# Third batch onward in one stated order for all engines, with a third PSUM bank for the first product and squares on ScalarE

## The chip, the cores and the metric

The kernel runs on one core of a Trainium2 chip. The metric is the device time of one execution in microseconds (us), the median of several runs. The engines are TensorE (PE; its weight loads are listed apart as PEld), VectorE (DVE), ScalarE (ACT), GpSimd (POOL) and SyncE (SP, which issues nearly all DMAs). Each executes its own instructions strictly in order and waits on semaphores for the others.

## What is computed

```python
q_s = softmax of q over the head dimension; k_s = softmax of k over the sequence
kv  = einsum('bhsd,bhse->bhde', k_s, v)
x   = einsum('bhsd,bhde->bhse', q_s, kv), heads side by side    # 4608 x 512
h   = x @ w_in;  g = relu(h) ** 2                               # 4608 x 2048
out = g @ w_out                                                 # 4608 x 512
```

The sizes are 8 batches, 8 heads, 576 positions, head dimension 64, all in fp32.

## The kernel before

**Tiling.** The 4608 rows of x are nine blocks of 512: 512 positions of each of the eight batches (blocks 0 to 7), and 64 left over of each batch, collected in block 8. A batch's eight heads are four pairs of two. Attention for a batch runs while the block before it is multiplied. Every fp32 product is made of three: both operands are split into a high and a low part (`copy` to fp32r on ScalarE, subtraction of the copy on GpSimd or VectorE), and high x high, high x low, low x high are added in PSUM.

**Blocks 0 and 1** take the first product as it stands (`h_part`), then relu, square, split (`relu`, `square`, `g_high`, `g_low`) and the second product (`out_part`). The order in block 0 is a list of tokens (`ORDER`). In block 1 a loop over 32 half steps runs `ffn_h` and `ffn_out`, and `put(at, ...)` hangs other work on half steps; only emission order is given, and a scheduler sorts the instructions of each engine from there on (`e.free()`).

**Blocks 2 to 8** use Strassen's scheme (Winograd's form) for the first product: eight *beats* a block, in each of which a 256-column pair of feature chunks is made of seven products (`PRODUCTS`), each six matmuls of 128x256. Their left sides are sums of w_in, made in block 1 (`w_sums`), kept in DRAM as `w_prod`; 14 stay in SBUF and the rest come through a ring of four tiles of two products. Their right sides are sums of x (`x_sums`: quarters B11 to B22, sums T1 to T4), each split in two (`x_split`). Between the products stand the second product's groups `o` of three 128x512 matmuls (`out_part`), eight a beat, which use the g of one and two beats ago. `BEAT` is this order.

The seven products go into two banks: X (bank 1) takes A11, S2, S3, A22 one upon the other, Y (bank 3) takes a copy of X after A11, then A12, and afterwards S1 and S4:

```python
def added(dst):     # after S1 with c[1][:, 1], after S4 with c[0][:, 1]
    e.dve.tensor_tensor(dst, dst, Y, op=ALU.add)
    e.dve.scalar_tensor_tensor(out=dst, in0=dst, scalar=0.0, in1=dst, op0=ALU.max, op1=ALU.mult)
def squared(dst, ps):   # after A12 with c[0][:, 0], Y; after A22 with c[1][:, 0], X
    e.act.activation(dst, ps, AF.Relu)
    e.dve.tensor_tensor(dst, dst, dst, op=ALU.mult)
```

`parts` then splits c into g: a cast on ScalarE, a subtraction on GpSimd.

**Attention of a pair** (`attention`): `k_max` (maximum of k over the sequence, with transposes and small reductions, on VectorE), `k_sub`, `k_exp`; `q_sub`, `q_exp`, `q_norm` (maximum, subtraction, exponential, sum, division, all but the exponential on VectorE), then a transpose `tb`, which goes to DRAM (`bounce_out`, one DMA) and comes back reordered as qT (`bounce_in`, four DMAs); `kv` (small matmuls), `rs`, `rr`, `kf`, `kv_high`, `kv_low` (its division and split); `q_high` and `q_low` (split of qT, ScalarE and GpSimd); and four products `attn`, each one matmul into a PSUM bank, an ACT copy `xf` of one half and DVE adds that write `x_raw`. `next_bank("a")` alternates between banks 0 and 7 for these and for kv. From batch 2's third pair on the two pairs of a half block are set off at fixed half steps (`TWO_AT`). In blocks 2 to 8 the matmuls are chained in the order of emission; the other engines' instructions are placed by the scheduler.

Of the kernel before, what the change touches and what calls it, by code (L numbers as in the profile page):

```python
# [31 lines left out]
BEAT = "A11 o o S2 A12 o o S3 o S1 o A22 o S4 o".split()  # L32
X_LOW_DVE = ("T2", "T3", "T4"), ("T3", "B22")
# [90 lines left out]
def attention_ffn_kernel(ctx: ExitStack, tc: tile.TileContext, q, k, v, w_in, w_out, out):  # L124
# [285 lines left out]
    def attention(b, pr, two):  # L410
# [43 lines left out]
        def q_norm():  # L454
            qn = st["qn"]
            qv = qn.rearrange("p j h d -> p (j h) d")
            qs = attn_pool.tile([P, LOW * 2, 1], F32, name="qs", tag=f"qs{n % NB}")
# [8 lines left out]
            e.dve.tensor_tensor(qv, qv, qs.broadcast_to([P, LOW * 2, D]), op=ALU.mult)  # L466
# [64 lines left out]
        def attn(g0, nj, h):  # L531
            def go():
# [8 lines left out]
                e.act.copy(corr[half[h]], ps[HALF:])
                e.dve.tensor_tensor(x[half[h]], ps[:HALF, :, :HIGH], corr[half[h], :, :HIGH], op=ALU.add)
                if nj == LOW:
                    e.dve.tensor_tensor(left[half[h]], ps[:HALF, :, HIGH], corr[half[h], :, HIGH], op=ALU.add)
                if nj == LOW and h == 1:
                    dst = x_left[:, pr, b * LEFT : (b + 1) * LEFT].rearrange("p (g a) -> p g a", g=2)
                    e.sp.dma_start(dst, left)
# [426 lines left out]
```

## Time and profile before

| | us |
|---|---|
| median of 3 runs (lowest, highest) | 939.71 (937.15, 939.99) |
| the profiled execution, its own time | 940.78 |
| its span in the trace | 939.0 |
| blocks 0 and 1 | 0 to 237 |
| blocks 2 to 5 (attention for batches 3 to 6, and part of the next) | 237 to 659.7 |
| block 6 (attention for batch 7) | 659.7 to 752.6 |
| blocks 7 and 8 (no attention) | 752.6 to 925.8 |
| last second-product groups and stores | 925.8 to 939 |

A block starts with its first A11 product. All of the kernel's instructions are issued by one helper (line 104 there, line 148 after the change), so groups are told apart by their tiles: `bank<-x_T,wp` and `bank<-x_B,wp` are the seven products (T1 to T4, and quarters of x), `bank<-wo,g` the second product, `bank<-vt,kt` the kv matmuls, `bank<-qs,kvs` the attention products, `c` and `g` what becomes of the first product, `qn`, `m`, `kt`, `xf`, `x_raw` steps of attention. A row of a stretch has its length in us, then for PE, PEld, DVE, ACT and POOL the busy us and the number of instructions, the mean granted share of TensorE's clock, the mean share of the DMA engines and GB/s. A row of a timeline has start and length in us, engine, operation, `out<-in`, size, count, and in brackets the idle time before it with its releaser. Matmuls overlap in the trace, so a PE row is longer than its share of PE's time.

### The profile page before, as it was taken

To read this page: it belongs to the slowest core of one execution; us is meant where nothing else is said; L and a number is where in the kernel's file an instruction comes from. 1 tells how busy PE (TensorE), PEld (TensorE's weight loads), DVE (VectorE), ACT (ScalarE), POOL (GpSimd) and SP (SyncE) were. 2 spreads that over 40 slices of the span, in tenths; PEclk is the share of its full clock that TensorE was granted. 3 is DMA by queue.
4 is the path that set the end of the run, shared out by engine and by line. 5 is a ranking of instruction groups with operands and counts; after the bars stand their busy time and mean duration, and the time that the engine had idled before them with its cause. 6 is when DMAs were issued, how large, how long until landed. Compare 5 with 4: busy or idle time off the path is not lost.

```text
span 939.0 us, 15774 instructions
## 1 busy us (share of the span) xinstructions
PE 870.0 (93%) x5422; PEld 733.5 (78%) x5422; DVE 674.5 (72%) x1392; ACT 454.4 (48%) x981; POOL 416.2 (44%) x350
## 2 busy tenths in 40 slices
PE   8999999997888988989899988988899999999998
PEld 6787878775777877877777777877788888888886
DVE  7998889889986789587877789597875553243332
ACT  4888845544653545445453545444544432243232
POOL 4577746667441363325341463326343432252222
PEclk9999999998899999999999999999999999999999
DMA  9989529877766744676466754676456544552552
GB/s 218 267 222 296 144 62 286 280 225 246 206 170 200 215 139 117 194 217 186 136 171 188 223 144 117 198 225 186 125 164 187 165 129 141 174 157 68 178 164 62
DMA packets 131663, 168.82 MB, mean 180 GB/s; under 512 B 51200, under 2 KB 95232, under 8 KB 131328
## 3 DMA queue, kind: packets, MB, share of 16 engines
q1 hardware_dynamic: 130832, 166.87, 62.0%
q8 instruction: 43, 0.70, 0.3%
q10 hardware_dynamic: 752, 0.95, 0.3%
q14 instruction: 36, 0.29, 0.1%
HBM read 134.74 MB, written 33.03 MB: 179 GB/s over the span
## 4 chain that ended last, share of the span: by engine, by line
PE 45%; DVE 30%; DMA 11%; issue 6%; ACT 4%; SPq 2%; POOL 1%; DVEq 0%; ACTq 0%; POOLq 0%
PE bank L104 45%; DVE c L104 6%; DVE m L104 5%; DMA qt<-in_q_dram 5%; DVE x_raw L104 3%; DMA kt<-in_k_dram 2%; SPq L104 2%; DVE qn L104 2%; DVE qm L104 2%; DVE kt L104 1%; DVE tb L104 1%; DMA wp<-w_prod 1%; DMA vt<-in_v_dram 1%; DVE x_T L104 1%; DVE T L104 1%
## 5 line engine op out<-in xcount | busy, mean ns | idle before, releaser
L104 PE MATMUL bank<-wo,g 128*128 128x512 f32 x1344 | 366.7, 396 | 0.0
L104 POOL TENSOR_TENSOR g<-c,g 128x512 fp32r<-128x512 f32 x112 | 147.5, 1318 | 338.6 <-ACT g L104 263.4
L104 PEld LDWEIGHTS bank<-wo,g 128*128 128x128 f32 x1344 | 232.3, 190 | 29.8
L104 PEld LDWEIGHTS bank<-x_T,wp 128*128 128x128 f32 x1344 | 186.8, 189 | 59.5 <-ACT bank L104 39.8
L104 PE MATMUL bank<-x_T,wp 128*128 128x256 f32 x1344 | 201.6, 286 | 22.9 <-ACT bank L104 20.3
L104 PE MATMUL bank<-x_B,wp 128*128 128x256 f32 x1008 | 152.4, 287 | 27.6 <-DVE c L104 27.5
L104 PEld LDWEIGHTS bank<-x_B,wp 128*128 128x128 f32 x1008 | 138.6, 192 | 43.5 <-DVE c L104 36.3
L104 DVE TENSOR_TENSOR c<-c 128x256 f32<-128x256 f32 x112 | 62.4, 557 | 93.3 <-ACT c L104 89.6
L104 POOL TENSOR_TENSOR qs<-qT,qs 64x640 fp32r<-64x640 f32 x48 | 80.6, 1678 | 90.8 <-ACT qs L104 81.3
L104 ACT CAST g<-c 128x512 fp32r<-128x512 f32 x112 | 69.5, 620 | 104.4 <-DVE c L104 103.8
L104 ACT ACTIVATE c<-bank 128x256 f32<-128x256 f32 x112 | 42.9, 383 | 114.3 <-PE bank L104 113.9
L104 DVE TENSOR_TENSOR c<-c,bank 128x256 f32<-128x256 f32 x112 | 46.5, 415 | 66.3 <-PE bank L104 65.9
L104 PE MATMUL bank<-x_hi,wi 128*128 128x512 f32 x256 | 88.2, 402 | 0.1
L104 DVE SCALAR_TENSOR_TENSOR c<-c 128x256 f32<-128x256 f32 x112 | 83.9, 749 | 2.8
L104 ACT COPY c<-bank 128x256 f32<-128x256 f32 x112 | 41.5, 371 | 91.5 <-PE bank L104 75.8
L104 PE MATMUL bank<-wo,g_hi 128*128 128x512 f32 x256 | 81.3, 401 | 0.0
L104 PEld LDWEIGHTS bank<-x_hi,wi 128*128 128x128 f32 x256 | 48.6, 190 | 11.5 <-DVE r L104 0.8
L104 PEld LDWEIGHTS bank<-wo,g_hi 128*128 128x128 f32 x256 | 47.8, 192 | 10.1 <-ACT g_hi L104 0.4
L104 PE MATMUL bank<-x_lo,wi 128*128 128x512 f32 x128 | 50.4, 394 | 0.0
L104 PE MATMUL bank<-wo,g_lo 128*128 128x512 f32 x128 | 49.9, 395 | 0.0
L104 DVE TENSOR_REDUCE m<-kt 128x128 f32<-128x640 f32 x32 | 41.9, 1308 | 8.4 <-DMA kt<-in_k_dram 8.1
L104 DVE TENSOR_REDUCE qm<-qt 128x10 f32<-128x640 f32 x32 | 25.9, 810 | 27.1 <-DMA qt<-in_q_dram 26.9
(122 smaller groups left out, 1190.3 us busy)
## 6 DMA issues: line engine op xcount, KB each, us to landing
wp<-w_prod SPq DMA_DIRECT2D x130, 512.0 KB, 3.8
wp<-w_prod SPq DMA_DIRECT2D x44, 256.0 KB, 3.0
out_dram<-o SPq DMA_DIRECT2D x68, 128.0 KB, 2.4
raw_i<-in_moe_w_in_dram SPq DMA_DIRECT2D x16, 512.0 KB, 7.7
raw_o<-in_moe_w_out_dram SPq DMA_DIRECT2D x16, 512.0 KB, 7.1
w_prod<-w_sum SPq DMA_DIRECT2D x32, 256.0 KB, 3.0
bounce<-tb SPq DMA_DIRECT2D x24, 320.0 KB, 2.2
qT<-bounce SPq DMA_DIRECT2D x96, 80.0 KB, 3.2
```

Of the source, the lines that this page charges most:

```text
L104: ins = f(*args, **kwargs)
```

## The change

- `BLOCK` is a list of tokens that states, for one block, the order of everything, and all five engines are chained to it from block 2 on. `name.j` is a step of beat j, `name/p` a step of attention of pair p (for the next batch), `x:` a step of the sums of x (`T` a sum, `h` a high part, `l` a low part), `w` a ring load, `ev`/`st` the taking out and storing of a finished output tile, `L` a load; `+` belongs to the block after, `-` to the one before. `AHEAD` hangs the first steps of batch 3 on half steps of block 1.
- S1 and S4 go to a third bank Z (bank 7), and S4 moves behind the next beat's A11 and two groups `o`. kv and all four attention products of a pair, for batches 3 to 7, share bank 0.
- `added` and `squared` become: `a22` (add to c, DVE), `r22` and `q22` (relu and square on ScalarE); `a12` (DVE adds c to Z in PSUM), `r12` (relu, ScalarE), `m12` (c times Z, DVE); `r11` (relu, ScalarE), `m11` (c times Y, DVE); `r21`, `q21` (relu and square, ScalarE). In block 1 the squares of 14 of 16 chunks go to ScalarE.
- For pairs from batch 2's third on, q's subtraction and q's division move from VectorE to GpSimd; from block 3 on all low parts of x are on GpSimd (before, T3 and B22 were on VectorE).
- `w_prod` is laid out in the order of use, so that every ring load is one DMA.

```diff
-BEAT = "A11 o o S2 A12 o o S3 o S1 o A22 o S4 o".split()
-X_LOW_DVE = ("T2", "T3", "T4"), ("T3", "B22")
+BEAT = "A11 o o S4 S2 o A12 o S3 o S1 o A22 o o".split()
+X_LOW_DVE = ("T2", "T3", "T4")
+Z_BANK = 7
...
+BLOCK = """
...
+a22.1 kv/1 r21.1 o12.1 Lv/3 r22.1 kp/1 kr/1 q21.1 o13.1 kh/1 A11.2 q22.1 kl/1 o00.2 c1.2 B/1 h1.1 o01.2 l1.1 S4.1
+Lk/3 S2.2 a12.1 qd/2 o02.2 r12.1 w4 u2.2 m12.1 A12.2 qh0/1 km/2 o03.2 Lq/0+ qh1/1 ql0/1 S3.2 k1/2 qx/2 o10.2 w5 h0.1
...
+P3/1 o02.3 u2.3 c3/1 A12.3 r12.2 d3/1 B/2 m12.2 o03.3 r11.3 x:T1 h0.2 S3.3 qm/3 l0.2 o10.3 w8 u3.3 m11.3 S1.3 qd/3
+qh0/2 kv/2 w9 a22.3 qh1/2 o11.3 Lv/0+ kr/2 A22.3 r22.3 ql0/2 kh/2 o12.3 o13.3 r21.3 Lq/1+ kl/2 kp/2 qx/3 A11.4 ql1/2
...
+""".split()
...
     def next_bank(who):
+        if who == "z":
+            return rest[2]
...
-            e.dve.tensor_tensor(
+            (e.pool if two else e.dve).tensor_tensor(
                 st["qn"].rearrange("p j h d -> p h j d"), qq, qm.broadcast_to([P, 2, LOW, D]), op=ALU.subtract
             )
...
-            e.dve.tensor_tensor(qv, qv, qs.broadcast_to([P, LOW * 2, D]), op=ALU.mult)
+
+        def q_scale():
+            qv, qs = st["qn"].rearrange("p j h d -> p (j h) d"), st["qs"]
+            (e.pool if two else e.dve).tensor_tensor(qv, qv, qs.broadcast_to([P, LOW * 2, D]), op=ALU.mult)
...
+            def times():
+                st[key] = next_bank("z" if b > 2 else "a")[:, : 2 * nj * BLK]
...
     def square(s):
         near = NFC <= s["blk"] * NFC + s["fc"] < NFC + LAG
+        if s["blk"] and not near:
+            e.act.activation(s["r"], s["r"], AF.Square)
+            return
...
+        def both(name):
+            return lambda: product(dict(A12=Y, S1=Z, S4=Z).get(name, X), j, name, name in ("A11", "S1"))
+
+        units = {name: both(name) for name in PRODUCTS}
+        units.update(
+            c1=lambda: e.act.copy(Y, X),
...
+            a22=lambda: e.dve.tensor_tensor(c(1)[:, 1], c(1)[:, 1], Z, op=ALU.add),
+            r22=lambda: relu(1, 1, c(1)[:, 1]),
+            q22=lambda: square(1, 1),
...
+            a12=lambda: e.dve.tensor_tensor(Z, Z, c(0)[:, 1], op=ALU.add),
+            r12=lambda: relu(0, 1, Z),
+            m12=lambda: times(0, 1, Z),
...
-    e.pe.last, e.pe.chained = None, True
...
+    for x in e.all:
+        x.last, x.chained = None, True
+    for blk in range(2, B + 2):
+        for token in BLOCK:
+            if blk <= B or token[-1] == "-" or token[0] == "o" or token[:2] in ("ev", "st"):
+                run(blk, token)
```

**PE, at the border of two beats with attention.** Banks 90, 92 and 96 are X, Y and Z (7); 89 is bank 0; `x_B_2576` and `x_B_2558` are B22, the right side of S4. Before, from S1 to the next S2:

```order
L104 MATMUL bank_92<-x_T_2574,wp 128x256 x6
L104 MATMUL bank_95<-wo_1254,g 128x512 x3
L104 MATMUL bank_90<-x_T_2575,wp 128x256 x6
L104 MATMUL bank_93<-wo_1254,g 128x512 x3
L104 MATMUL bank_92<-x_B_2576,wp 128x256 x6
L104 MATMUL bank_94<-wo_1254,g 128x512 x3
L104 MATMUL bank_96<-qs_3408,kvs_677 128x320
L104 MATMUL bank_89<-qs_3410,kvs_677 128x320
L104 MATMUL bank_90<-x_B_2570,wp 128x256 x6
L104 MATMUL bank_91<-wo_1101,g 128x512 x3
L104 MATMUL bank_95<-wo_1101,g 128x512 x3
L104 MATMUL bank_90<-x_T_2571,wp 128x256 x6
```

Now, from A22 and the next A11 past S4 to S2:

```order
L148 MATMUL bank_90<-x_T_2557,wp 128x256 x6
L148 MATMUL bank_93<-wo_944,g 128x512 x3
L148 MATMUL bank_94<-wo_944,g 128x512 x3
L148 MATMUL bank_90<-x_B_2552,wp 128x256 x6
L148 MATMUL bank_91<-wo_866,g 128x512 x3
L148 MATMUL bank_95<-wo_866,g 128x512 x3
L148 MATMUL bank_89<-qs_4285,kvs 128x320
L148 MATMUL bank_96<-x_B_2558,wp 128x256 x6
L148 MATMUL bank_90<-x_T_2553,wp 128x256 x6
L148 MATMUL bank_93<-wo_866,g 128x512 x3
L148 MATMUL bank_92<-x_B_2554,wp 128x256 x6
L148 MATMUL bank_89<-qs_4300,kvs 128x320
```

S4 stands behind the next A11 instead of ahead of it, in a bank of its own with S1 (which stands three rows ahead of this piece's first, with a kv and a second-product group between); the two attention products of a half, which stood side by side in banks 7 and 0, stand four groups apart in bank 0.

**DVE, beats 3 and 4 of block 4.** Before, from the key maximum to the add that releases S4:

```order
L104 TENSOR_REDUCE m<-kt_78 128x128
L104 STREAM_TRANSPOSE mt<-m 128x128
L104 TENSOR_REDUCE mp<-mt 128x4
L104 STREAM_TRANSPOSE tb<-qn 128x5x4x32
L104 TENSOR_REDUCE m_5666<-mp 32x4 x4
L104 TENSOR_TENSOR x_raw<-bank_96,xf 64x2x4x32
L104 TENSOR_TENSOR xf<-bank_96,xf 64x2x32
L104 TENSOR_TENSOR x_raw<-bank_89,xf 64x2x4x32
L104 TENSOR_TENSOR xf<-bank_89,xf 64x2x32
L104 TENSOR_TENSOR qn<-qt_82,qm 128x2x5x64
L104 TENSOR_REDUCE m_5671<-m_5666 32x4 x2
L104 TENSOR_TENSOR c_5448<-c_5448,bank_92 128x256
```

Now, from the add after S1 (`a22.3`) to the add after S4 (`a12.3`), which lies in the next beat:

```order
L148 TENSOR_TENSOR c_5410<-c_5410,bank_96 128x256
L148 TENSOR_SCALAR rs<-bank_89 128x1
L148 RECIPROCAL rs<-rs 128x1
L148 TENSOR_SCALAR kf<-bank_89,rs 128x64
L148 TENSOR_TENSOR kvs<-kf,kvs 64x64 x2
L148 TENSOR_REDUCE sums_680<-qn 128x10
L148 TENSOR_REDUCE qs<-sums_680 128x10
L148 RECIPROCAL qs<-qs 128x10
L148 TENSOR_REDUCE m<-kt_79 128x128
L148 TENSOR_TENSOR x_raw<-bank_89,xf 64x2x4x32
L148 TENSOR_TENSOR xf<-bank_89,xf 64x2x32
L148 TENSOR_TENSOR bank_96<-bank_96,c_5373 128x256
```

The add after S1 now stands ahead of the pair's steps instead of behind a key maximum, and the subtraction of q is no longer in DVE's list.

**ACT, beat 3 of a block, around the casts that read the bounced q of pair 2.** Now:

```order
L148 COPY c_4274<-bank_90 128x256
L148 CAST qs_4285<-qT 64x640
L148 CAST qs_4300<-qT 64x640
L148 ACTIVATE c_4274<-c_4274 128x256
L148 CAST kvs<-kf 64x64 x4
L148 ACTIVATE c_4274<-bank_90 128x256
```

The last row is `r21`, the relu of X, behind which the next A11 may write X; before the change its place was the scheduler's.

## Rows read from the trace of the kernel before

**Rows 1.** page of the profile, span and busy time of each engine

```profile
span 939.0 us, 15774 instructions
...
PE 870.0 (93%) x5422; PEld 733.5 (78%) x5422; DVE 674.5 (72%) x1392; ACT 454.4 (48%) x981; POOL 416.2 (44%) x350
```

**Rows 2.** stretches: us, busy PE, PEld, DVE, ACT, POOL, clock, DMA

```profile
132.00:237.00 105.00, 95.25 (x485) 75.62 (x483) 95.00 (x188) 52.72 (x104) 68.51 (x62) 0.96 0.77 245
237.00:659.70 422.70, 375.60 (x2488) 321.89 (x2485) 335.99 (x741) 201.65 (x457) 175.63 (x134) 0.98 0.63 178
659.70:752.60 92.90, 90.05 (x586) 78.77 (x585) 63.27 (x140) 43.93 (x106) 36.90 (x31) 1.00 0.57 164
752.60:925.80 173.20, 172.03 (x1055) 150.44 (x1054) 63.76 (x107) 55.25 (x125) 50.18 (x38) 1.00 0.47 137
```

**Rows 3.** waits of PE and DVE, 237 to 659.7 us: total, times, longest

```profile
PE bank L104 <- DVE c L104: 25.1, 17, 2.7
PE bank L104 <- ACT bank L104: 19.1, 22, 1.8
...
DVE qm L104 <- DMA qt<-in_q_dram: 23.6, 8, 3.5
```

**Rows 4.** timeline, DVE then PE, beat 4 of block 4: start, us, work

```profile
506.88 1.31 DVE L104 TENSOR_REDUCE m<-kt 128x128 f32<-128x640 f32 x1 [0.90 <-DMA kt<-in_k_dram]
...
512.40 0.42 DVE L104 TENSOR_TENSOR c<-c,bank 128x256 f32<-128x256 f32 x1
...
512.87 0.98 PE L104 MATMUL bank<-x_B,wp 128*128 128x256 f32 x6 [1.94 <-DVE c L104]
```

**Rows 5.** timeline of POOL and DVE late in block 3

```profile
418.95 3.81 POOL L104 TENSOR_TENSOR qs<-qT,qs 64x640 fp32r<-64x640 f32 x2 [3.54 <-ACT qs L104]
...
421.27 1.79 DVE L104 SCALAR_TENSOR_TENSOR c<-c 128x256 f32<-128x256 f32 x1
...
423.75 0.42 DVE L104 SCALAR_TENSOR_TENSOR c<-c 128x256 f32<-128x256 f32 x1
```

**Rows 6.** timeline of PE, ACT and PEld, one beat of block 8

```profile
861.48 0.87 PE L104 MATMUL bank<-x_B,wp 128*128 128x256 f32 x6
...
863.34 0.37 ACT L104 COPY bank<-bank 128x256 f32<-128x256 f32 x1
...
863.75 0.77 PEld L104 LDWEIGHTS bank<-x_T,wp 128*128 128x128 f32 x6 [0.44 <-ACT bank L104]
...
866.67 0.88 PE L104 MATMUL bank<-x_T,wp 128*128 128x256 f32 x6
...
872.30 0.87 PE L104 MATMUL bank<-x_B,wp 128*128 128x256 f32 x6
```

**Rows 7.** timeline, one pair's bounce: issue on SP, cast that reads it

```profile
518.52 1.75 SPq L104 DMA_DIRECT2D qT<-bounce  x4
...
522.30 1.48 ACT L104 CAST qs<-qT 64x640 fp32r<-64x640 f32 x2 [0.89 <-DMA qT<-bounce]
```

**Rows 8.** groups, 237 to 659.7 us: xcount | busy us, mean ns | idle

```profile
L104 POOL TENSOR_TENSOR g<-c,g 128x512 fp32r<-128x512 f32 x63 | 82.9, 1315 | 170.2 <-ACT g L104 114.1 <-PE bank L104 38.5 <-issue 16.8
...
L104 DVE SCALAR_TENSOR_TENSOR c<-c 128x256 f32<-128x256 f32 x64 | 44.6, 697 | 1.3
...
L104 ACT ACTIVATE c<-bank 128x256 f32<-128x256 f32 x64 | 24.5, 383 | 55.6 <-PE bank L104 55.4
...
L104 POOL TENSOR_TENSOR x_T<-T,x_T 128x512 fp32r<-128x512 f32 x12 | 19.5, 1641 | 0.0
...
L104 PE MATMUL bank<-vt,kt 128*64 128x65 f32 x323 | 13.1, 243 | 0.0
```

**Rows 9.** groups, whole execution: a q step of the first batches on POOL

```profile
L104 POOL TENSOR_TENSOR qn<-qt,qm 128x640 f32<-128x640 f32 x8 | 10.1, 1262 | 8.1 <-DVE qm L104 8.1
```

**Rows 10.** 132 to 237 us: a wait of PE, and block 1's squares

```profile
PE bank L104 <- DVE x_raw L104: 3.9, 2, 3.6
...
L104 DVE TENSOR_TENSOR r<-r,bank 128x512 f32<-128x512 f32 x14 | 9.4, 671 | 1.0 <-ACT r L104 1.0
```

More of the change, by code (lines that the diff above doesn't have):

```diff
@@ L529, in k_pad, with parts, view, x_part @@
             e.pool.memset(kk[HALF:, :, HIGH, :], -FLT_MAX)
[L531 to L532 removed]
+        def parts(g0, nj, h):
+            key = g0, h
+            def view(ps):
+                return ps.rearrange("p (g j a) -> p g j a", g=2, a=BLK)
+            def x_part():
+                return x_raw(b)[:, pr].rearrange("p (j g a) -> p g j a", g=4, a=BLK)[:, g0 : g0 + 2]
+            def times():
+                st[key] = next_bank("z" if b > 2 else "a")[:, : 2 * nj * BLK]
+                qs = st["q"][h][:, g0 : g0 + 2, :nj].rearrange("p g j a -> p g (j a)")
+                e.pe.matmul(view(st[key]).rearrange("p g j a -> p g (j a)"), kvs[:, h], qs, start=True, stop=True)
+            def copy():
@@ L540, in go @@
-                e.pe.matmul(ps.rearrange("p g j a -> p g (j a)"), kvs[:, h], qs, start=True, stop=True)
-                e.act.copy(corr[half[h]], ps[HALF:])
-                e.dve.tensor_tensor(x[half[h]], ps[:HALF, :, :HIGH], corr[half[h], :, :HIGH], op=ALU.add)
-                if nj == LOW:
[L544 to L547, printed above, removed]
+                e.act.copy(st[g0][half[h], :, :nj], view(st[key])[HALF:])
@@ new lines, in add, with keep_left @@
+            def add():
+                ps, xf = view(st[key]), st[g0]
+                corr, left = xf[half[h], :, :nj], xf[half[h], :, LOW]
+                e.dve.tensor_tensor(x_part()[half[h]], ps[:HALF, :, :HIGH], corr[:, :, :HIGH], op=ALU.add)
+                if nj == LOW:
+                    e.dve.tensor_tensor(left, ps[:HALF, :, HIGH], corr[:, :, HIGH], op=ALU.add)
+            return times, copy, add
+        def keep_left():
+            dst = x_left[:, pr, b * LEFT : (b + 1) * LEFT].rearrange("p (g a) -> p g a", g=2)
+            e.sp.dma_start(dst, st[0][:, :, LOW])
@@ L674, in w_sums @@
         for name, src in names:
-            e.sp.dma_start(w_prod[j, :, w_at[name]], src.bitcast(F32))
+            pair, place = divmod(w_at[j, name], 2)
+            e.sp.dma_start(w_prod[pair, :, place], src.bitcast(F32))
     held, loaded = {}, {}
@@ L938, in attention_ffn_kernel, with refill @@
-    prev = None
-    for u in todo:
-        with ExitStack() as order:
-            if prev is not None:
-                order.enter_context(tc.issue_after(prev.ins))
-            prev = u()
+    ring = (len(USED) - KEPT) // 2
+    def refill(blk, n):
+        if blk <= B:
+            at = (blk - 2) * ring + n
+            load_products(KEPT + 2 * n, 2, f"i{RING[at % len(RING)]}", stay)
+    for n in range(len(RING)):
+        refill(2, n)
+    blocks = {(blk, j): strassen(j) for blk in range(2, B + 1) for j in range(NPR)}
```

330 lines of the change are left out of this document (200 added, 130 removed).

## The prediction

> **What bounds the kernel now.** I read the page first, then the stretches, the waits of TensorE, and two timelines. The page [rows 1] has TensorE busy for 870.0 of 939.0 us, so at most some 70 us can be won without changing its work. The stretches [rows 2] say where: blocks 2 to 5 (237 to 659.7 us) last 422.7 us with PE busy for 375.6, an idle time of 47.1 us; block 6 lasts 92.9 us against 105.7 in the mean of the four before it, and has the same products with a VectorE that is busy for 63.3 us instead of 84.0; blocks 7 and 8, which have no attention left, last 86.6 each. So TensorE falls back exactly where VectorE is full. The waits [rows 3] name the place: 25.1 us on DVE's c and 19.1 us on ACT's bank, 44.2 of the 47.1. Both are bank 3 (Y). S4 may not write Y before DVE's `added` has read S1 out of it, and the copy of X into Y (on which S2 waits) may not start before `added` has read S4. The timeline [rows 4] shows why that read is late: DVE stands in line with a key maximum that waits for its load, fourteen more attention instructions follow, and the add that S4 waits for starts at 512.40; PE loses 1.94 us there. Another 23.6 us of DVE's time [rows 3] is waiting for q loads, with everything behind it in the queue.
>
> Even blocks 7 and 8 are not at the floor. In a beat of block 8 [rows 6] eight groups (a product, or three second-product matmuls) go from 866.67 to 872.30, 0.704 us each, so 15 groups need 10.56 us; the beat takes 10.82, because S2 waits for the copy into Y, which starts at 863.34 only.
>
> **The change, part by part.** *Third bank, S4 moved.* S1 and S4 go to Z. Between S1 and S4 there are now seven groups (4.9 us) instead of three, and between A11 and S2 three instead of two (2.1 us for a copy of 0.37 us [rows 6]). The next S1 waits for a12, r12 and m12 after S4: an add, a relu and a multiply. a12 writes to PSUM and has no row; the nearest is the add that reads PSUM, 0.42 us [rows 4], and with 0.38 for the relu [rows 8] the three take some 1.5 us with their hand-overs, in six groups (4.2 us). I cost the three waits at nothing; what hides them is this distance, and if an engine runs over a beat late, they return.
>
> *What TensorE then needs.* A block without attention: 8 x 10.56 = 84.5 us. Attention adds the difference of PE's busy time between block 6 (90.05) and the mean of 7 and 8 (86.0), 4.0 us, and the two groups of kv matmuls that fall ahead of block 6's window: 13.1 us for 16 pairs [rows 8] is 0.82 us each, 1.6. So blocks 3 to 5 need 90.2 us each, block 2 87.4 (four second-product groups fewer), block 6 89.4 (one kv group fewer), blocks 7 and 8 169.0 together: 616.4 against 688.8 now, **72.4 us less at the floor**.
>
> *Can the others keep up?* VectorE, 84.0 us a block, loses 16 scalar_tensor_tensor of 0.697 us [rows 8] = 11.2, the two q steps of four pairs (8 x about 1.05, between the 0.42 of a short one and POOL's 1.262 [rows 5, 9]) = 8, and two x parts of 1.6 or so; some 62 us remain, as in block 6. The 23.6 us of waiting for q loads go too: the table has `Lq` two beats or more ahead of `qm`. ScalarE, 50.4 us, gets two relus and two squares a beat, 32 x 0.383 [rows 8] = 12.3, so 63. The square has no row: the nearest is the relu of its shape at 0.383, and I take that; a fifth more would add 1.2 us to an engine with 27 free. GpSimd, 43.9 us, gets 8 x 1.262 [rows 9] = 10.1 and two x parts of 1.641 [rows 8] = 3.3, so 57. Each is busy for 63 to 70% of 90 us. The order of ScalarE still has a single ACT_TABLE_LOAD, so the squares bring no table loads.
>
> *What is still late.* (a) The bounce. From the first issue of its four loads to the cast it takes 522.30 - 518.52 = 3.78 us, and ACT stood idle for it [rows 7]. In the new order four PE groups, 2.8 us, lie between `B` and `qh0` for three of the four pairs. ACT, now in stated order, waits 1.0 us there, and behind it stand casts and the relu of X on which the next A11 waits. That relu has two groups (1.4 us) for itself; less 0.38 for it and some 0.3 for the two hand-overs, 0.7 us is spare. So 0.3 to 1.0 us of each of 20 pairs reach PE; I take 0.5: 10 us (bounds 0 and 20). (b) GpSimd in beat 0: a memset, five x parts and two g parts, 0.2 + 5 x 1.641 + 2 x 1.315 [rows 8] = 11.0 us in a beat of 10.7. The first `d` of the next beat overwrites x_raw and waits for the last of them; I allow 1 us in each of five blocks (bounds 0 and 2). So 57.4 of the 72.4 are left.
>
> The Trainium skill, "SBUF — State Buffer", section "SBUF: two separate sides", says that VectorE and GpSimd hold a shared port pair exclusively, and that a VectorE instruction with two SBUF inputs waits until a GpSimd instruction that reads SBUF is through, and the reverse. The rows agree: while POOL ran from 418.95 to 422.76, a DVE instruction that takes 0.42 us alone took 1.79 [rows 5]. By this rule work handed to GpSimd comes back as waits of both: an x part (1.641) costs 0.33 more than a g part of the same shape (1.315), and if no such waits existed beat 0 would hold only 9.4 us of GpSimd's work and (b) would be 0, a total 5 us lower than mine. I keep (b).
>
> *Block 1 (132 to 237 us).* PE is idle for 9.75 us of 105, with DVE busy for 95.0 [rows 2]. 14 squares of 0.671 us [rows 10] leave DVE, and the second pair of batch 3 is prepared later; GpSimd gains some ten q steps, 12.6 us on 68.5. One PE wait there, 3.9 us for DVE to empty the attention bank [rows 10], is at the entry to block 2 and stays in kind. Half the idle time, 5 us (bounds 0 and 9.75). Ring loads and output stores move on SP's queue but keep their number and bytes; they are hidden now and each stays a full ring slot ahead of its use: nothing. If that cover goes, PE waits on wp, which it does not now.
>
> Sum: 57.4 + 5 = 62.4 us off the profiled execution's 940.78 us (its span is 1.8 us shorter) is 878.4. The median of the three runs, 939.71, is 1.1 below that execution, so I predict **877 us**.
>
> **The rivals.** *Floor:* (a) and (b) are absorbed and block 1 gives all it has: 939.7 - 72.4 - 9.75 = 858 us. For it: block 6 already shows that a freed DVE suffices. Against it: the late cast of (a) is in the rows.
>
> *Half given back:* the order was laid out for durations that the chip does not keep, and in-order engines pass each lateness on: (a) 20 us, (b) 10, 2 us a block from hand-overs at kv and the entry, 10, and nothing from block 1. 939.7 - 32.4 = 907 us. For it: before, a scheduler's order had the same engines and PE still waited 44 us; against it: nothing in the new order is closer than some 1 us except (a) and (b).
>
> *Slower, the single attention bank:* kv and the four attention products of a pair now share bank 0, where before they alternated between 0 and 7. Each must wait until DVE has added the last one out, behind whatever stands in DVE's queue. That is five hand-overs a pair, 100 in five blocks; each needs an ACT copy and one or two DVE adds, about 1.1 us from the nearest rows (0.383 and 0.697) [rows 8]. The order leaves two to four groups, 1.4 to 2.8 us, so 0.3 us or more are spare. It decides when the mean wait passes 62.4 / 100 = 0.62 us; at 1.0 us each the kernel takes 877 + 100 = 977. For it: such a wait has cost PE up to 3.6 us [rows 10]. Against it: DVE has 27 of 90 us free.
>
> That the change does not do what it says is excluded by its order: the 112 scalar_tensor_tensor are gone, and S1 and S4 stand on bank 96 (Z).
>
> **How the numbers follow.** Forecast (865 to 892 us) 0.55, floor (below) 0.14, half given back (892 to 930) 0.20, between that and no change 0.01. About 0.3%, 2.8 us either way, is what a measurement can tell here: no change 0.02, slower by more, the single bank or several lesser things with it, 0.08. Faster is the sum of the first four, 0.90. The range from 856 to 912 us holds the forecast, the floor, and the lower 0.12 of half given back, 0.81.
>
> **What would show it.** Right: blocks 3 to 5 last 90 to 95 us; PE's waits on DVE's c and ACT's bank fall from 44.2 us in blocks 2 to 5 below 5; DVE is busy for about 62 us a block, ACT 63, POOL 57; beats of blocks 7 and 8 last 10.56 us; ACT's wait on qT grows, with some PE waits on ACT behind it. Wrong: PE waits on DVE's x_raw or xf at bank 0 of 60 us or more (the slower rival), PE waits on wp, or blocks 3 to 5 at 100 us or more with none of the engines full.

## The result and the profile after

The changed kernel takes 872.99 us (median of 4 runs, 870.37 to 875.45), the kernel before on the same chip 939.85 (4 runs). The ratio is 0.9291, 95% interval 0.9256 to 0.9326. The forecast was 877 us, in a range from 856 to 912. The profiled execution, the fastest of the four, has a span of 868.1 us against 939.0. The page, to be read beside [rows 1]:

```profile
span 868.1 us, 15842 instructions
...
PE 847.6 (98%) x5422; PEld 735.1 (85%) x5422; DVE 512.2 (59%) x1210; ACT 538.4 (62%) x1219; POOL 475.4 (55%) x406
```

PE's idle time fell from 69.0 to 20.5 us. That is 48.5 of the 70.9 us that the span lost; the other 22.4 are PE's own busy time, for the same 5422 matmuls. The stretches (block 1 from 132 us on, blocks 2 to 6, blocks 7 and 8), to be read beside [rows 2]. Block 2 is cut at its first A11. The later cuts stand some 2.2 us behind a block's first A11, at the S4 of the block before, so that every block still has 56 products; block 2's stretch then holds two second-product groups (1.4 us) of block 3:

```profile
132.00:224.80 92.80, 90.63 (x463) 74.13 (x461) 73.31 (x139) 57.28 (x111) 75.30 (x66) 0.98 0.84 267
224.80:324.40 99.60, 91.26 (x622) 81.04 (x619) 67.11 (x170) 64.00 (x154) 50.45 (x43) 0.97 0.70 210
324.40:416.30 91.90, 90.86 (x626) 80.72 (x625) 58.93 (x158) 60.52 (x146) 53.42 (x44) 1.00 0.69 201
416.30:506.70 90.40, 90.40 (x626) 80.65 (x625) 58.05 (x158) 60.53 (x146) 53.56 (x43) 1.00 0.71 204
506.70:597.40 90.70, 90.70 (x626) 80.67 (x624) 57.89 (x159) 60.65 (x146) 53.62 (x43) 1.00 0.70 204
597.40:687.00 89.60, 89.60 (x606) 80.09 (x605) 49.54 (x134) 57.90 (x139) 51.67 (x42) 1.00 0.58 175
687.00:855.90 168.90, 168.90 (x1058) 152.40 (x1057) 31.37 (x72) 76.16 (x187) 53.80 (x42) 1.00 0.45 141
```

In us, before and after: block 1's stretch 105.0 and 92.8; blocks 2 to 5 422.7 and 372.6; block 6 92.9 and 89.6; blocks 7 and 8 173.2 and 168.9; the tail 13.2 and 12.2. That is 12.2 + 50.1 + 3.3 + 4.3 + 1.0 = 70.9. (By equal work blocks 2 to 5 gave 1.4 more and the tail 1.4 less.) From block 4 on PE is busy without a gap. The waits of PE from 240 us to the end of block 6, beside [rows 3], are two, of 1.0 us together:

```profile
PE bank L148 <- ACT c L148: 0.7, 1, 0.7
PE bank L148 <- ACT bank L148: 0.3, 1, 0.3
```

The same place as [rows 4], beat 4 of block 4, in DVE's timeline (start, us, work, and in brackets the idle time before it):

```profile
461.21 1.26 DVE L148 TENSOR_REDUCE m<-kt 128x128 f32<-128x640 f32 x1
...
462.86 0.41 DVE L148 TENSOR_TENSOR bank<-bank,c 128x256 f32<-128x256 f32 x1
...
464.49 0.42 DVE L148 TENSOR_TENSOR c<-c,bank 128x256 f32<-128x256 f32 x1
...
473.53 0.43 DVE L148 TENSOR_TENSOR bank<-bank,c 128x256 f32<-128x256 f32 x1 [2.64 <-PE bank L148]
```

The key maximum is still there, but its load is in, only two short adds of attention stand between it and the add after S4, and a beat later DVE waits for PE where PE had waited for DVE.

**One stall is new**, at the entry to block 2 (timeline of ACT, DVE and PE):

```profile
226.05 0.62 ACT L148 CAST w_sum<-a 128x512 fp32r<-128x512 f32 x1 [2.19 <-POOL a L148]
...
226.05 1.75 DVE L148 TENSOR_TENSOR T<-x_raw 128x512 f32<-128x512 f32 x1 [1.86 <-POOL a L148]
227.72 1.75 DVE L148 TENSOR_TENSOR w_sum<-a,w_sum 128x512 fp32r<-128x512 f32 x1
229.39 1.74 DVE L148 TENSOR_TENSOR x_raw<-x_raw 128x512 f32<-128x512 f32 x1
...
234.12 0.69 DVE L148 TENSOR_TENSOR x_T<-T,x_T 128x512 fp32r<-128x512 f32 x1
...
234.40 0.36 ACT L148 COPY bank<-bank 128x256 f32<-128x256 f32 x1
...
234.82 1.44 PE L148 MATMUL bank<-x_T,wp 128*128 128x256 f32 x5 [8.32 <-ACT bank L148]
```

PE is through with the first A11 and a group behind it at 226.5 and stands for 8.32 us until the copy into Y. The copy itself has what it needs; it stands in ScalarE's order behind the casts of x's sums, these behind DVE's subtractions, and those behind the last sum of w. DVE's operations of 128x512 take 1.74 us there while GpSimd works beside them, and 0.69 at 234.12, when GpSimd has stopped.

### The profile page after: what moved, and what is told of

Same layout as the page of the kernel before. It is cut to its first block, busy times and chain, and to the rows that moved or that the text cites. A ratio compares the mean times of both kernels' runs of the same rounds, so it can differ in the third digit from the quotient of the medians.

```text
span 868.1 us, 15842 instructions
## 1 busy us (share of the span) xinstructions
PE 847.6 (98%) x5422; PEld 735.1 (85%) x5422; DVE 512.2 (59%) x1210; ACT 538.4 (62%) x1219; POOL 475.4 (55%) x406
## 4 chain that ended last, share of the span: by engine, by line
PE 83%; DVE 5%; DMA 5%; issue 2%; ACT 2%; POOL 2%; SPq 1%; ACTq 0%; POOLq 0%; DVEq 0%
PE bank L148 83%; SPq L148 1%; DMA vt<-in_v_dram 1%; DMA w_prod<-w_sum 1%; DVE w_sum L148 1%; DVE m L148 1%; DMA qT<-bounce 1%; DMA bounce<-tb 1%; DMA qt<-in_q_dram 1%; POOL qn L148 0%; POOL qs L148 0%; DMA wp<-w_prod 0%; DMA w_prod<-wi 0%; DVE qn L148 0%; ACT qn L148 0%
## 5 line engine op out<-in xcount | busy, mean ns | idle before, releaser
L148 PE MATMUL bank<-x_T,wp 128*128 128x256 f32 x1344 | 197.5, 283 | 8.6 <-ACT bank L148 8.6
L148 PE MATMUL bank<-x_B,wp 128*128 128x256 f32 x1008 | 148.5, 283 | 0.8 <-ACT c L148 0.7
L148 DVE TENSOR_TENSOR c<-c,bank 128x256 f32<-128x256 f32 x168 | 67.6, 415 | 109.2 <-PE bank L148 58.4
L148 ACT ACTIVATE c<-bank 128x256 f32<-128x256 f32 x168 | 64.7, 385 | 90.5 <-PE bank L148 75.2
L148 DVE TENSOR_TENSOR bank<-bank,c 128x256 f32<-128x256 f32 x56 | 23.9, 426 | 108.0 <-PE bank L148 108.0
L148 ACT ACTIVATE c<-c 128x256 f32<-128x256 f32 x168 | 66.7, 414 | 14.7 <-DVE c L148 12.4
L148 DVE TENSOR_TENSOR x_raw<-bank,xf 64x256 f32<-64x256 f32 x96 | 39.6, 412 | 34.1 <-ACT xf L148 31.0
L148 PEld LDWEIGHTS bank<-x_hi,wi 128*128 128x128 f32 x256 | 48.4, 189 | 10.8 <-DVE x_lo L148 0.4
L148 POOL TENSOR_TENSOR qn<-qn,qs 128x640 f32<-128x640 f32 x30 | 40.2, 1340 | 24.9 <-DVE qs L148 12.2
L148 ACT COPY xf<-bank 64x320 f32<-64x320 f32 (+1 forms) x96 | 38.0, 396 | 23.9 <-PE bank L148 22.0
L148 ACT CAST qs<-qT 64x640 fp32r<-64x640 f32 x48 | 34.8, 726 | 28.3 <-DMA qT<-bounce 27.7
```

The lines of the kernel that those rows point to most:

```text
L148: ins = f(*args, **kwargs)
```

## The experiments

Medians in us; the ratio is to runs of the kernel before on the same chip, with its 95% interval. "Relief" is VectorE's: squares to ScalarE, q steps and x's low parts to GpSimd. TensorE is in a stated order from block 2 on in every run: that of the kernel before in before, e1 and e9, that of `BLOCK` in the others.

| run | product banks | attention banks | DVE, ACT, POOL in | relief | us | ratio |
|---|---|---|---|---|---|---|
| before | 2 | 2 | scheduler's order | no | 939.85 | 1 |
| e1 | 2 | 2 | scheduler's order | yes | 894.05 | 0.9519 (0.9476, 0.9562) |
| e9 | 2 | 1 | scheduler's order | yes | 980.58 | 1.0423 (1.0401, 1.0445) |
| e4 | 3 | 1 | scheduler's order | yes | 918.17 | 0.9767 (0.9722, 0.9813) |
| e2 | 3 | 1 | stated order | in part | 889.94 | 0.9471 (0.9421, 0.9521) |
| e12 | 2 | 1 | stated order | yes | 880.14 | 0.9361 (0.9329, 0.9392) |
| the change | 3 | 1 | stated order | yes | 872.99 | 0.9291 (0.9256, 0.9326) |

**e1, relief alone.** The kernel before with these edits:

```diff
 def added(dst):
-    e.dve.scalar_tensor_tensor(out=dst, in0=dst, scalar=0.0, in1=dst, op0=ALU.max, op1=ALU.mult)
+    e.act.activation(dst, dst, AF.Relu)
+    e.act.activation(dst, dst, AF.Square)
 def squared(dst, ps):
-    e.dve.tensor_tensor(dst, dst, dst, op=ALU.mult)
+    e.act.activation(dst, dst, AF.Square)
 # q's subtraction and division, of pairs two by two
-    e.dve.tensor_tensor(
+    (e.pool if two else e.dve).tensor_tensor(
-X_LOW_DVE = ("T2", "T3", "T4"), ("T3", "B22")
+X_LOW_DVE = ("T2", "T3", "T4"), ()
```

> The kernel before, with only the relief of VectorE: from block 2 on the relu and square of the sums go to ScalarE as two instructions, the square of the other two quarters too, q's subtraction and division of the later pairs go to GpSimd, and all low parts of x. Two banks, S4 ahead of the next A11, and the scheduler's order stay. Theory bank (the gain comes from the third bank and the later S4, which put four to seven groups between a product and the reader of its bank): the waits at Y stay in kind, S4 behind the add after S1, the copy into Y behind the add after S4; blocks 3 to 5 last 97 us or more, the total is 905 to 930. Rival relief (the waits came from VectorE's 84 us a block alone): with some 60 us a block they go, blocks 3 to 5 last 90 to 93, the total is 885 or less.

894.05 us, between the two ranges. Blocks 3 to 5 last 94.5, 98.1 and 95.7 us, block 3 with DVE busy for 57.7, and PE's waits at Y, 44.2 us in [rows 3], are under half, the entry to block 2 aside (PE's waits from 240 us to the end of block 6, then block 3 as a stretch):

```profile
PE bank L104 <- DVE c L104: 15.8, 9, 2.4
PE bank L104 <- ACT bank L104: 4.3, 4, 1.6
```

```profile
334.80:429.30 94.50, 91.01 (x627) 79.96 (x625) 57.71 (x143) 67.64 (x162) 54.62 (x44) 1.00 0.68 195
```

So 45 us (939.14 for the kernel before on the same chip) come with an emptier VectorE queue, with two banks and S4 where it was; the scheduler sorts the engines anew around the moved work, and e1 does not keep the two apart. In blocks 7 and 8 this kernel's beats take 10.55 us, as the changed kernel's do: two banks are no limit there.

**e2, part of VectorE's work given back** in the changed kernel:

```diff
-r22=lambda: relu(1, 1, c(1)[:, 1]),
-q22=lambda: square(1, 1),
+r22=lambda: e.dve.scalar_tensor_tensor(out=c(1)[:, 1], in0=c(1)[:, 1], scalar=0.0, in1=c(1)[:, 1], op0=ALU.max, op1=ALU.mult),
+q22=lambda: None,
-q21=lambda: square(1, 0),
+q21=lambda: times(1, 0, c(1)[:, 0]),
-(e.pool if two else e.dve).tensor_tensor(
+e.dve.tensor_tensor(
-low(name[1:], e.pool)
+low(name[1:], e.dve if name[1:] in ("T3", "B22") else e.pool)
```

> The changed kernel with VectorE's work of blocks 2 to 8 given back: one scalar_tensor_tensor in place of relu and square (0.70 us, 8 a block), the square of the fourth quarter on DVE, q's subtraction and division on DVE, the low parts of T3 and B22 on DVE. Three banks and the stated order stay. DVE's 58 us a block become some 77. Theory bank: PE does not notice, 870 to 885 us, PE's waits in blocks 3 to 5 below 2 us a block. Rival relief: the waits come back with DVE's load, 905 us or more.

889.94, between the ranges again: 17 us come back. DVE is busy for 73 of 94.3 us a block, where the change has 58 and the kernel before 84.0, so some 15 of the 26 us of relief were given back. What PE waits for most is the attention bank (240 to 700 us):

```profile
PE bank L148 <- DVE xf L148: 6.6, 13, 0.8
PE bank L148 <- ACT g L148: 3.2, 5, 0.6
```

**e4, the scheduler's order for all but TensorE:**

```diff
-    for x in e.all:
-        x.last, x.chained = None, True
+    e.pe.last, e.pe.chained = None, True
```

> The changed kernel with TensorE alone in stated order from block 2 on; DVE, ACT, POOL and SP are sorted by the scheduler, as before the change. Banks, engines and the order of emission stay. Theory bank: the distances on PE hold whatever the others' order, 870 to 885 us. Rival order (the waits go because adds and relus stand ahead of attention steps in the queues): PE waits for DVE or ACT by 5 us a block or more, 900 us or more.

918.17, in the rival's range: 45 us of the gain are lost, though banks, engines and PE's order are those of the change. PE waits for ScalarE's relus and copies and for the attention bank (240 to 700 us):

```profile
PE bank L148 <- ACT c L148: 18.0, 20, 2.7
PE bank L148 <- DVE xf L148: 14.0, 16, 1.7
```

**e9, a single attention bank in a scheduler's order,** the slower rival by itself, put into e1:

```diff
-    ps = next_bank("a")...
+    ps = next_bank("z" if b > 2 else "a")...
-    ... kv=lambda: kv(next_bank("a")), ...
+    ... kv=lambda: kv(next_bank("z" if b > 2 else "a")), ...
```

> As e1_before_relief (two product banks, the scheduler's order, VectorE relieved; 894.1 us), but for batches 3 to 7 kv and all attention products of a pair share bank 0, as in the changed kernel. It prices the slower rival of the prediction by itself, in a scheduler's order. Theory (without a stated order a single attention bank costs what the run with TensorE alone in stated order showed as PE's waits for DVE's xf, 14.0 us, and more through what stands behind them): 906 to 925 us, with PE waits on DVE x_raw or xf of 10 us or more. Rival (a light VectorE empties the bank in time in any order): 890 to 898.

980.58, 86.5 us slower than e1 and far outside the theory's range. The kv of both pairs of a half block goes to bank 0 before either is divided, so the first pair's kv is overwritten and e9 does not compute the kernel's output. The number of operations is unchanged, and its time prices the hand-overs that are left; what a kernel that keeps both kv would take is not shown. PE's waits (240 to 760 us):

```profile
PE bank L104 <- DVE xf L104: 42.1, 18, 4.2
PE bank L104 <- DVE x_raw L104: 32.4, 18, 3.6
```

Over the prediction's 100 hand-overs that is 0.87 us each, past the 0.62 at which this rival decides. The mechanism is real; in the changed kernel the stated order of the other engines keeps it from PE, which waits 14.0 us for xf in e4 and not at all in the change, with the same banks and the same order on PE.

**e3, e10, e11: two product banks in a stated order, badly placed.** In e3, S4 goes to Y ahead of the next A11, with its three steps behind it; in e10 the add goes into c, so that Y is free after it; e11 is e10 with attention on banks 0 and 7:

```diff
 # e3
-X, Y, Z = (banks[i][:, :HN] for i in (*H_BANKS, Z_BANK))
+X, Y, Z = (banks[i][:, :HN] for i in (*H_BANKS, H_BANKS[1]))
-... A22.2 ... o12.2 w6 r21.2 ... o13.2 q21.2 A11.3 a22.2 ... S4.2 ... S2.3 ... a12.2 ... r12.2 ... m12.2
+... a22.2 ... A22.2 ... o12.2 S4.2 a12.2 r12.2 m12.2 w6 r21.2 ... o13.2 q21.2 A11.3 ... S2.3
 # e10, on top of e3
-a12=lambda: e.dve.tensor_tensor(Z, Z, c(0)[:, 1], op=ALU.add),
-r12=lambda: relu(0, 1, Z),
-m12=lambda: times(0, 1, Z),
-m11=lambda: times(0, 0, Y),
+a12=lambda: e.dve.tensor_tensor(c(0)[:, 1], c(0)[:, 1], Z, op=ALU.add),
+r12=lambda: relu(0, 1, c(0)[:, 1]),
+m12=lambda: square(0, 1),
+m11=lambda: square(0, 0),
 # e11, on top of e10 (kv and attention)
-... next_bank("z" if b > 2 else "a") ...
+... next_bank("a") ...
```

> The changed kernel with S1 and S4 in Y again: S4 stands two groups ahead of the next A11 with its add, relu and multiply right behind it, the steps on Y ahead of S1; the squares on ScalarE, the q steps on GpSimd and the stated order stay. After S4 an add, a relu, a multiply and the copy into Y (0.43 + 0.39 + 0.43 + 0.36 us and four hand-overs) must pass in the four groups (2.8 us) ahead of S2, with attention steps in the queues between. Theory bank: S2 waits for the copy, 0.3 to 0.6 us a beat, blocks 3 to 5 last 93 to 96 us, the total is 890 to 905. Rival order or relief (two banks would do in a stated order with a light VectorE): 868 to 880.

> As e3_after_two_banks (S1 and S4 in Y under the stated order; 940.6 us), but Y is free after one instruction that reads it: the add after S4 goes into c instead of into PSUM, relu and square then read c, and the quarter after A12 is relu from Y and a square of c on ScalarE. Theory occupancy (the third bank is needed because the changed kernel's add, relu and multiply all read the bank, 1.3 us and hand-overs; a form that frees Y after one add fits two banks): 875 to 895 us, beats of blocks 7 and 8 at 10.55. Rival (two banks are too few in a stated order at any occupancy): 915 or more.

> As e10_two_banks_short, with bank 7, which is then free, given back to attention: kv and the attention products alternate between banks 0 and 7 as before the change. If e10 still waits for DVE's x_raw or xf, those waits go and the total is 2 to 10 us below e10's. If the single attention bank costs nothing in a stated order, it is within 3 us of e10.

940.56, 951.28 and 940.25 us (ratios 1.0016, 1.0119 and 0.9997): the whole gain is gone in each, and e10, which frees Y sooner than e3, is slower. The theories of e3 and e10 missed; e10 lies in its rival's range, whose reason e12 refutes below. e11 is 11 us below e10, just past the 2 to 10 expected. A beat of e10's block 8, where no attention is left, tells why (timeline of DVE, ACT and PE):

```profile
873.43 0.87 PE L148 MATMUL bank<-x_B,wp 128*128 128x256 f32 x6
...
874.41 0.42 DVE L148 TENSOR_TENSOR c<-c,bank 128x256 f32<-128x256 f32 x1 [2.36 <-PE bank L148]
874.87 0.86 ACT L148 ACTIVATE c<-c 128x256 f32<-128x256 f32 x2 [4.37 <-DVE c L148]
875.64 0.36 ACT L148 ACTIVATE c<-bank 128x256 f32<-128x256 f32 x1
...
876.05 0.98 PE L148 MATMUL bank<-x_B,wp 128*128 128x256 f32 x6 [1.05 <-ACT c L148]
```

The product at 873.43 is S4. ScalarE stands idle for 4.37 us until DVE has added it, does relu and square of that sum, and only then, at 875.64, the relu of X, whose input has been there since A22 ended at about 872.9 and for which the next A11 waits. I had put `r12` and `m12` ahead of `r21`: the loss is at X, not at Y. In e3 `m12` is VectorE's, so that only `r12` stands ahead on ScalarE, and a beat of its block 8 takes 11.28 us instead of 11.87: that is why e10 is the slower one there. In beat 1, the one beat where `r21` stands ahead of them by chance, block 8 takes 10.65 us from A11 to A11; in the others 11.9. These runs say nothing of the banks, but they price one misplaced pair of instructions: 1.2 us a beat. Between e10 and e11 the second attention bank is worth 11 us, so a single one does cost where the rest runs late.

**e12, two product banks, well placed.** The forms of e10, but ScalarE keeps the changed kernel's order (but for `r11.7`, ahead of S1.7):

```diff
-... A22.2 ... o12.2 w6 r21.2 ... o13.2 q21.2 A11.3 a22.2 ... S4.2 ... S2.3 ... a12.2 ... r12.2 ... m12.2
+... a22.2 ... A22.2 ... o12.2 S4.2 w6 r21.2 ... o13.2 a12.2 q21.2 A11.3 ... S2.3 ... r12.2 ... m12.2
```

> Two product banks under the stated order once more, since in e3_after_two_banks and e10_two_banks_short the relu and square of the sum after S4 stood ahead of the relu of X (r21) in ScalarE's order, so that the next A11 waited for them. Here ScalarE keeps the order of the changed kernel but for one relu (r11.7, moved ahead of S1.7), S4 stands one group ahead of the next A11's predecessor, its add into c (DVE) behind the next group, and relu and square read c; attention keeps the single bank 0, bank 7 is unused. Theory placement (VectorE's relief and the stated order bring the gain, and a bank freed by one add leaves two groups ahead of the copy into Y): 870 to 885 us, beats of block 8 at 10.55. Rival bank (a third product bank is needed in a stated order whatever the placement): 900 or more, with PE waits on ACT's bank (the copy into Y).

880.14 us, in the theory's range, with beats of 10.54 us in block 8. The entry wait of block 2 aside (9.1 us, 8.3 in the change), PE's waits in 240 to 687 us are small, and none is for the copy into Y:

```profile
PE bank L148 <- POOL qs L148: 2.2, 4, 0.8
PE bank L148 <- ACT c L148: 1.2, 3, 0.8
PE bank L148 <- DVE x_raw L148: 1.0, 5, 0.2
PE bank L148 <- DVE xf L148: 0.7, 2, 0.5
```

So in a stated order with VectorE relieved the third bank, with the placement and the forms that go with it, is worth about 7 of the 67 us; the intervals of e12 and the change don't meet. They are not waits for Y. By the profiled executions, 11.6 us apart, block 2 is 5.1 us longer in e12 and blocks 3 to 6 together 6.1, counted from A11 to A11; what makes them so is open. Two cells were not run: a stated order with VectorE's full load of before, and the new layout of `w_prod` by itself (PE waits for wp in neither kernel).

**e5, no lead for the bounced q.** `qh0` and `qh1` stand directly behind `B`, for all pairs but the first of batch 3:

```diff
-... B/2 m12.2 ... S1.3 qd/3 qh0/2 kv/2 w9 a22.3 qh1/2 ...
+... B/2 qh0/2 qh1/2 m12.2 ... S1.3 qd/3 kv/2 w9 a22.3 ...
```

> The changed kernel with the two casts of the bounced q (qh0, qh1) directly behind the issue of its loads in ScalarE's order, instead of four groups later; all else stays. Theory distance (four groups of lead were enough, because the loads took 2.4 to 3.4 us from issue to cast and the products had two groups to spare): ScalarE now stands 2.5 us or more at each of some 20 pairs, with relus, copies and casts behind it, and PE waits for ACT by 0.5 to 1.5 us a pair: 883 to 903 us. Rival (ScalarE, busy for 60 of 90 us, catches up before any product needs it): 871 to 876.

962.09 us (ratio 1.0214, 1.0172 to 1.0255): 89 us slower than the change, three to nine times the theory's price. One pair in the timeline of ACT and PE, then PE's stretches around it:

```profile
368.50 1.47 ACT L148 CAST qs<-qT 64x640 fp32r<-64x640 f32 x2 [3.65 <-DMA qT<-bounce]
...
371.21 0.98 PE L148 MATMUL bank<-x_T,wp 128*128 128x256 f32 x6 [1.84 <-ACT c L148]
...
374.93 0.64 PE L148 MATMUL bank<-qs,kvs 128*128 128x320 f32 x1 [1.70 <-POOL qs L148]
375.37 1.48 PE L148 MATMUL bank<-x_T,wp 128*128 128x256 f32 x6
```

```profile
364.70:371.20 6.50, 4.68 (x29) 3.86 (x28) 0.70 (x2) 2.76 (x6) 0.44 (x1) 1.00 0.70 176
371.20:374.90 3.70, 2.01 (x9) 1.25 (x9) 3.45 (x13) 1.51 (x3) 3.60 (x3) 0.66 0.24 86
374.90:380.70 5.80, 5.77 (x23) 5.26 (x24) 3.89 (x12) 2.06 (x6) 4.62 (x3) 0.63 0.51 145
380.70:385.00 4.30, 4.30 (x30) 3.91 (x30) 1.72 (x4) 2.94 (x7) 1.29 (x1) 1.00 0.61 202
```

ScalarE's wait of 3.65 us becomes one of PE (1.84), the copies and casts behind it make GpSimd late, and PE waits again (1.70). The granted clock is 1.00 until 372 us, 0.50 (the lower of its two levels, 1.2 GHz) from 373 to 379 and 1.00 again from 380: it falls after the first wait, before the second begins. Its means over the two stretches, 9.5 us together, are 0.66 and 0.63, and six matmuls take 1.48 us, elsewhere 0.87. Blocks 3 to 5 (343.1 to 673.7 us) show both parts: 330.6 us instead of 273.0, of which PE's idle time is 37.9 instead of 1.0, and its busy time 292.7 instead of 272.0 for the same 1874 matmuls, at a mean granted clock of 0.93 instead of 1.00.

**e6, block 1's squares back on VectorE; e7 and e8, sums of w in more tiles, and sooner:**

```diff
 # e6
-        if s["blk"] and not near:
-            e.act.activation(s["r"], s["r"], AF.Square)
-            return
 # e7
-        both = const.tile([P, 2, 2, 2, HN], F32R, name="w_sum", tag="x_lo0")
+        if j < 2:
+            both = const.tile([P, 2, 2, 2, HN], F32R, name="w_sum", tag="x_lo0")
+            both = both[:, 0], both[:, 1]
+        else:
+            both = [stay.tile([P, 2, 2, HN], F32R, name="w_sum", tag=f"i{2 * j - 4 + n}") for n in range(2)]
 # e8, on top of e7
-        put(2 * (NFC + LAG) + 3 * j, lambda j=j: w_sums(j))
+        put(2 * (NFC + LAG) + 5 * j // 2, lambda j=j: w_sums(j))
```

> The changed kernel with the squares of block 1 back on VectorE (14 of 0.67 us). Theory entry chain (block 1's matmuls ended 12 us earlier, but PE then stood 8.3 us at the first copy into Y, behind the sums of w and x, so what the squares gave is mostly given back there): block 1's last matmul moves 4 to 10 us later, the wait shrinks by nearly as much, the total is 872 to 878. Rival (the squares are worth their own time on the path): 880 to 886.

> The changed kernel with the sums of w from the third on in SBUF tiles of w_in chunks no longer needed, two sums earlier, instead of all eight in one tile, so that a sum does not wait for the DMA that takes the sum before it to DRAM. Theory entry chain, single tile (the last sum of w is late because its casts wait for that DMA, and x's sums and the first copy into Y stand behind it in order): PE's wait of 8.3 us at the entry to block 2 falls to 2 to 5, the total is 867 to 870. Rival (the sums are late because GpSimd and VectorE, or the DMA itself, are full): the wait stays, 871 to 876.

> As e7_wsum_buffers, and the sums of w are hung on every fifth half of a half step instead of every third half step (two and a half half steps apart), so that the last comes 3.5 half steps, some 10 us, earlier in the order of emission. Theory entry chain, single tile: the last sum and the sums of x end before block 1's last product, the entry wait is below 2 us, block 1 itself is 0 to 3 us longer since VectorE's lows of g stand behind the sums, the total is 864 to 869. Rival (engines or DMA full): block 1 grows by as much as the wait shrinks, 871 to 877.

e6: 874.66 us (0.9294, 0.9274 to 0.9315), in the theory's range and not to be told from the change, but not by the theory's mechanism. Block 2 begins 2.8 us later, at 227.6, not 4 to 10, and the entry wait is 7.6 us instead of 8.3: the 9.4 us of squares [rows 10] cost block 1 little, and little of that is given back at the entry. e7: 870.39 (0.9246, 0.9222 to 0.9270); the entry wait falls to 2.15 us as expected, but block 2 begins at 228.5 instead of 224.8, and the total is at the border of the two ranges. In e7's timeline of DVE and PE:

```profile
226.57 1.78 DVE L148 TENSOR_TENSOR x_T<-T,x_T 128x512 fp32r<-128x512 f32 x1
...
228.89 0.68 DVE L148 TENSOR_TENSOR x_T<-T,x_T 128x512 fp32r<-128x512 f32 x1
...
232.88 0.98 PE L148 MATMUL bank<-x_T,wp 128*128 128x256 f32 x6 [2.15 <-ACT bank L148]
```

e8: 870.07 (0.9245, 0.9225 to 0.9266), above its theory's range and equal to e7. PE's wait for the copy is gone there, and one of 1.46 us for VectorE's low part of g stands in its place; block 2 begins at 228.6. The single tile did hold up the sums, but in e7 some 3.7 of the 6.2 us that it cost at the entry reappear inside block 1. Both medians are the lowest of this study, 2.6 and 2.9 us below the change, but the intervals overlap with the change's; whether they beat it is open.

## Why the prediction came out right, step by step

**The floor: right.** It is the forecast without (a), (b) and block 1. Blocks 3 to 5 were forecast to need 90.2 us each, 270.6; they last 91.9, 90.4 and 90.7, 273.0. Block 6: 89.4 and 89.6. Blocks 7 and 8: 169.0 and 168.9. The count of groups times the pace of a few that follow each other without a wait [rows 6] gave blocks 3 to 8 together to 0.5%. The sentence ahead of it, that the page's idle time leaves at most some 70 us, was no such bound: a third of the gain is in PE's busy time. That time holds part of the waits, since six matmuls behind a wait are a row of 0.98 us instead of 0.87 [rows 4, 6], and part of the clock, which was 0.96, 0.98, 0.98 and 1.00 in blocks 2 to 5 before.

**(a), the bounce: mechanism right, size wrong.** "So 0.3 to 1.0 us of each of 20 pairs reach PE; I take 0.5: 10 us": PE's waits on ACT come to 1.0 us in all. ACT does wait for qT, 27.7 us in 23 waits from 224.8 to 687 us, as forecast. The step that failed is the spare of 0.7 us set against a wait of 1.0. In beat 3 of block 4 (timeline of SP, ACT and PE):

```profile
452.66 1.75 SPq L148 DMA_DIRECT2D qT<-bounce  x4
...
456.09 1.48 ACT L148 CAST qs<-qT 64x640 fp32r<-64x640 f32 x2 [1.23 <-DMA qT<-bounce]
...
457.34 0.87 PE L148 MATMUL bank<-x_T,wp 128*128 128x256 f32 x6
...
458.85 0.37 ACT L148 ACTIVATE c<-bank 128x256 f32<-128x256 f32 x1
...
459.44 0.87 PE L148 MATMUL bank<-x_B,wp 128*128 128x256 f32 x6
```

The casts are over at 457.57, before A22 (the product at 457.34) has given the relu of X its input; ScalarE comes to that relu at 458.85, is through at 459.22, and A11 follows at 459.44 without a wait. Some 0.2 us remain spare: ScalarE's wait falls into time in which it has nothing to do for A11 yet. The 0.3 us that I took for two hand-overs had no row; in e10 A11 starts 0.05 us behind the end of that relu (876.00, 876.05). e5 shows that beyond it the price is not 0.5 us a pair but 4.7 (89 us over the 19 pairs moved).

**(b), GpSimd in beat 0: size wrong, and not on PE's path.** The 5 us were to appear as PE waiting through x_raw; no such wait is in PE's list. What I mis-sized is the x part, 1.641 us. Groups of GpSimd from 240 us to the end of block 6, and a wait of DVE there:

```profile
L148 POOL TENSOR_TENSOR x_B<-x_raw,x_B 128x512 fp32r<-128x512 f32 x14 | 20.5, 1466 | 1.5 <-ACT x_B L148 0.9
...
L148 POOL TENSOR_TENSOR x_T<-T,x_T 128x512 fp32r<-128x512 f32 x14 | 17.9, 1291 | 0.0
```

```profile
DVE x_raw L148 <- POOL x_B L148: 2.1, 4, 0.5
```

With these, two parts of quarters, three of sums and two of g (1.295 each) make an estimated 9.6 us in a beat of 10.55, not 11.0: GpSimd does not run over. What is left of the wait, 2.1 us in all, stays with DVE. The port rule of the Trainium skill ("SBUF — State Buffer", section "SBUF: two separate sides") is borne out again, by the DVE row of 0.68 us that takes 1.78 beside GpSimd in e7; but it cost time at the entry to block 2, where DVE is on the path, and not in beat 0.

**Block 1 and the entry: the step that failed.** "Half the idle time, 5 us" was 12.2 (7.6 of idle time, the rest busy time), and "One PE wait there, 3.9 us for DVE to empty the attention bank, is at the entry to block 2 and stays in kind" was wrong in size and kind: the wait is 8.32 us, for the copy into Y. I let PE come earlier without asking what else had to be ready by then: the sums of w and x, on GpSimd, VectorE and one tile. So block 2's stretch lasts 99.6 us, of which 1.4 are block 3's, not 87.4. Of the 10.8 us too many 8.3 are the wait; some 1.9 are the clock, by an estimate: it is at 0.50 when PE starts again at 234.82 and until about 238.6, 3.7 us for what takes half of that at 1.00. e7 bears this out in part: of 6.2 us less wait, 3.7 come back as a later start of block 2.

These misses cancel, and that the sum came out so near is luck: blocks 2 to 8 gave 59.1 us (57.7 and block 3's 1.4) where 57.4 were forecast, with 10.8 more lost in block 2 and nearly all of the 15 of (a) and (b) saved.

**The loads** were near: DVE 58 us a block (forecast 62), ACT 60.5 (63), POOL 53.5 (57). The square takes 0.413 us, 8% more than the relu's 0.383 that I took for it.

**The cause, only half right.** I read the waits of [rows 3] as a matter of bank Y, with VectorE's queue as the reason for the late reads, and put the third bank first. The runs turn this round: relief by itself gives 45 us, the stated order of DVE, ACT, POOL and SP 45 (e4 against the change), some 15 of the 26 us a block of relief under the stated order still 17, and the third bank, with what goes with it, 7. They are not parts of a sum: a stated order makes the distances that a light VectorE can keep. Here the row that named the bank said where the wait ended, not what would remove it.

**The slower rival** was sound in mechanism and near in price, 0.87 us a hand-over in e9 where it took 1.0. That e9's 980.58 us lie so close to its 977 is luck: one is 86.5 on top of e1's 894, the other 100 on top of 877. "Against it: DVE has 27 of 90 us free" was not the reason it failed to come: in e9 DVE is as free. The stated order is.

## What to carry to other kernels

A wait that is named after a buffer is often a queue's: before adding buffers, take work out of the queue of the engine that frees them, and see how much of the wait goes. In an in-order schedule ask of each instruction that may wait which instruction behind it another engine needs; in e10 a pair of steps on the wrong side of a relu cost about as much as the whole change had won (e12, where ScalarE's order is put right, is 71 us faster). And when a stage ends earlier, list what else must be ready at its end: the next stall waits there.

## What was not expected of the hardware

A stall of PE can cost more than its length, and the length alone does not tell when. In e5 a wait of 1.84 us was followed by some 6.8 us at a granted clock of 0.50; behind the 8.32 us at the entry to block 2 it was 0.82 over 10.2 us, and behind e12's 9.13 it was 0.74 over 10.1. But behind e7's 2.15 us it stayed at 1.00 over 10.2, and in e10, where PE waits for ScalarE's relu 30 times in 237 to 687 us, 1.1 us at the longest, it is 1.00 over that stretch too. In blocks 4 and 5 of the changed kernel, where PE has no gap, it stays at 1.00.
